# The order of 1,866 steps from a written list, and a last output tile in two column halves

## The chip, the cores and the metric

The kernel runs on one core of a Trainium2 chip. The metric is the device time of one execution in microseconds (us). Three executions of the kernel before took 486.77, 487.08 and 488.17 us; the median, 487.08 us, is the number that the prediction is about.

## What is computed

A gated linear recurrence, and behind it a two-layer block with the Mish activation. All data are float32.

```python
f = 1.0 / (1.0 + np.exp(-f_logit))                 # q, k, v, f_logit: (4, 8, 768, 48)
for t in range(S):
    state = f[:, :, t, :, None] * state + np.einsum('bhd,bhe->bhde', k[:, :, t], v[:, :, t])
    y[:, :, t] = np.einsum('bhd,bhde->bhe', q[:, :, t], state)
x = y.transpose(0, 2, 1, 3).reshape(3072, 384)
h = x @ w_in                                        # 384 x 2048
g = h * np.tanh(np.log1p(np.exp(np.minimum(h, 20.0))))
out = g @ w_out                                     # 2048 x 384
```

## The kernel before, in words

**The recurrence** is cut into 24 chunks (n0 to n23): 6 stretches of 128 time steps for each of 4 batches. A chunk is loaded on SP's queue (log-gates `l`, keys and queries `kq`, values `v`), prepared (L439 to L462: gates to running sums, their exponentials, and the products of k and q with them), and then goes through four stages: scores (L495) and masks (L508), a transposed copy of k called `kt`, the update of the state (L561), and the outputs (L632, L645). For the first eight chunks `kt` comes from TensorE transposes (L527) and a copy by ScalarE (L543). From chunk n8 on it goes by DMA: VectorE transposes blocks (L531), four DMAs write them to HBM (L536, `kd<-inv`), one reads them back (L538, `kt<-kd`), and one TensorE step, the run of that chunk (L595), does update, scores and outputs together.

**The two layers** work on 6 groups of 512 tokens (four chunks each) and 16 slices of 128 hidden columns: 96 units u0 to u95. A unit is nine 128x512 matmuls into `h` (`moe_in`, L256), eight elementwise steps on ScalarE, VectorE and GpSimd (`mish`, L270 to L278), and nine matmuls into the three output tiles `o0`, `o1`, `o2` (`moe_out`, L283). Every product is done as high and low parts, hence three matmuls for each. The weights of slice j are loaded (`raw`, 768 KB) and split into the parts `wh` and `wl` by ScalarE (L388, L395) and VectorE (L390 to L396).

**The order.** No engine's order is written in the loops. Each piece of work is entered with `add` as a step: its engine, a planned cost, what it reads and writes. There are 1,863 steps. `Plan.order` gives each a rank, shifts ranks at random with 71 listed seeds, and packs the steps by rank (`pack`); the steps are then issued in the order of their planned starts. So the order of instructions on TensorE (PE), VectorE (DVE), ScalarE (ACT), GpSimd (POOL) and of the DMAs on SP's queue comes out of that plan, and each engine works through its own list strictly in order. `Plan.issue` also puts filler matmuls (L376, on zeros) where the planned start of a TensorE step is more than 527 ns after the end of the one before it, up to the first `moe_out`.

**The end.** In the last unit, u95, each output tile gets its three matmuls (684 ns planned), then one copy to SBUF that multiplies by -2, by VectorE for tiles 0 and 2 (L797) and by ScalarE for tile 1 (L793), and one DMA of 256 KB (L799). The plan before puts tile 1 last.

Of the kernel before, what the change touches and what calls it, by code (L numbers as in the profile page):

```python
# [2 lines left out]

# [10 lines left out]
AF = mybir.ActivationFunctionType  # L14
ALU = mybir.AluOpType
# [4 lines left out]
P = 128  # L20
# [7 lines left out]
GT = GC * C  # L28
NG = NT // GT
NF = DFF // P  # L30
NK = DM // P
# [7 lines left out]
TURNS = [(0, 0, 8), (1, 0, 8), (0, 8, 16), (1, 8, 16)]  # L39

LEAD = [(-2, 8), (22, 32)]
SEEDS = [
# [8 lines left out]
]  # L51
BASE = (300.0, 20.0, 7)
NR = 3
LAG = 2
TD = 8
# [5 lines left out]
SP_ISSUE = 470  # L61
# [4 lines left out]
class Plan:  # L66
# [28 lines left out]
        lag = self.LATENCY[engine] if lag is None else lag  # L95
        self.steps.append((engine, cost, issue, before, size, port or engine == "pool", lag))

    def pack(self, rank, ahead, haste, back=False):


        steps = self.steps
        count = len(steps)
        engine, cost, port = [s[0] for s in steps], [s[1] for s in steps], [s[5] for s in steps]
        before = [s[3] for s in steps]
        after = [[] for _ in steps]
        for i in range(count):
            for b in before[i]:
                after[b].append(i)
        if back:
            before, after = after, before  # L110
        free = dict.fromkeys(self.FREE, 0.0) if back else dict(self.FREE)
        queue = {e: [] for e in free}
        left, ready, start = [len(b) for b in before], [0.0] * count, [0.0] * count
        for i in range(count):
            if not left[i]:
                queue[engine[i]].append(i)
        transfers = shared = 0.0
        for _ in range(count):
            best = None
            for e, q in queue.items():  # L120
                if q:
                    at = [(max(ready[i], shared) if port[i] else ready[i], i) for i in q]
                    t0 = max(free[e], min(at)[0])
                    _, t, i = min(
                        (rank[i] + haste * max(0.0, r - t0), max(free[e], r), i)
                        for r, i in at if r <= t0 + ahead
                    )
                    if best is None or t < best[0]:
                        best = t, i
            t, i = best  # L130
            e = engine[i]
            queue[e].remove(i)
            start[i] = t
            end = free[e] = t + cost[i]
            if port[i]:
                shared = end
            if e == "sp" and not back:
                transfers = max(transfers, end + 650.0) + steps[i][4] / self.RATE
                end = transfers - 650.0
            for a in after[i]:  # L140
                f = a if back else i
                if engine[i] == engine[a] == "pe":
                    lag = 0.0
                else:
                    lag = steps[f][6]
                    if back and engine[f] == "sp":
                        lag += steps[f][4] / self.RATE
                ready[a] = max(ready[a], end + lag)
                left[a] -= 1
                if not left[a]:  # L150
                    queue[engine[a]].append(a)
        return start

    @staticmethod
    def nudge(rank, seed):
        pick = random.Random(seed)
        lo, hi = min(rank), max(rank)
        at = lo + (hi - lo) * pick.random() ** 2
        width = (1e3, 3e3, 1e4, 4e4)[seed % 4]
        spread = (150.0, 500.0, 1500.0, 5000.0)[seed // 4 % 4]  # L160
        part = (1.0, 0.3, 0.1, 0.03)[seed // 16 % 4]
        return [
            r + pick.gauss(0.0, spread) if abs(r - at) <= width and (part == 1.0 or pick.random() < part) else r
            for r in rank
        ]

    def order(self):
        count = len(self.steps)
        cost = [s[1] for s in self.steps]
        ahead, haste, turns = BASE  # L170
        rank = list(range(count))
        for _ in range(turns):
            start = self.pack(rank, ahead, haste)
            back = self.pack([-start[i] - cost[i] for i in range(count)], ahead, haste, True)
            rank = [-back[i] - cost[i] for i in range(count)]
        for seed in SEEDS:
            rank = self.nudge(rank, seed)
        self.start = self.pack(rank, ahead, haste)
        return sorted(range(count), key=lambda i: (self.start[i], i))

    def issue(self):
# [19 lines left out]
def T_ACT(n, psum=False, bias=0):  # L201
    return n / 1.2 + (50 if psum else 92) + 93 * bias + 2


def T_DVE(n):
    return n / 0.96 + 70
# [7 lines left out]
def recurrence_moe_kernel(  # L214
# [11 lines left out]
    nc = tc.nc  # L226
# [10 lines left out]
    wih, woh = wh[:, :, : NK * P], wh[:, :, NK * P :]  # L237
# [40 lines left out]
            ("pool", T_POOL(GT), 1, lambda: nc.gpsimd.tensor_tensor(gl, g, gh.bitcast(F32), ALU.subtract)),  # L278
        )

    def moe_out(o, m, gh, gl, j, first, last, woh=woh, wol=wol):
        for i, (w, x) in enumerate(((woh, gh), (wol, gh), (woh, gl))):
            nc.tensor.matmul(  # L283
                o, w[:, j, m * P : (m + 1) * P], x, start=(first and i == 0), stop=(last and i == 2)
            )


    with tc.tile_pool(name="work", bufs=1) as pool, tc.tile_pool(
# [35 lines left out]
        def lender(m):  # L324
            return pairs(("ob", m)) + (pairs(("l", NR)) if m == 0 else thirds(("kq"[m - 1], NR)))
# [440 lines left out]
        def out_unit(u):  # L766
            t, g, j = units[u]
            half = g < 2
            first, last = (j == x for x in (turns[t][1], turns[t][2] - 1))
            part = last and half and j == NF - 1  # L770
            gs = u % 3
            if part:
                for m in range(NK):
                    add("sp", SP_ISSUE, lambda m=m, g=g: nc.sync.dma_start(ob_[m], halves[g][m * P : (m + 1) * P, :]),
                        [("half", g, m)], lender(m), 262)
            if u == 0:
                plan.until = len(plan.steps)
            if last or first:
                for m in range(NK):
                    add("pe", 684, lambda m=m: moe_out(o_[m], m, gh_[gs], gl_[gs], j, first, last),  # L780
                        [("w", "h", j), ("w", "l", j), ("gh", gs), ("gl", gs)], [("o", m)])
            else:
                add("pe", 2042, lambda: [moe_out(o_[m], m, gh_[gs], gl_[gs], j, first, last) for m in range(NK)],
                    [("w", "h", j), ("w", "l", j), ("gh", gs), ("gl", gs)], [("o", m) for m in range(NK)])
            if last:
                dst = halves[g] if j < NF - 1 else out[:, g * GT : (g + 1) * GT]
                for m in range(NK):
                    if part:
                        add("dve", T_DVE(GT), lambda m=m: nc.vector.scalar_tensor_tensor(
                            ob_[m], o_[m], -2.0, ob_[m], ALU.mult, ALU.add),  # L790
                            [("o", m)], lender(m))
                    elif m == 1:
                        add("act", T_ACT(GT, True), lambda m=m: nc.scalar.activation(ob_[m], o_[m], AF.Copy, scale=-2.0),  # L793
                            [("o", m)], lender(m))
                    else:

                        add("dve", T_DVE(GT), lambda m=m: nc.vector.tensor_scalar(ob_[m], o_[m], -2.0, None, ALU.mult),  # L797
                            [("o", m)] + ["flag"] * (u == len(units) - 1), lender(m))
                    add("sp", SP_ISSUE, lambda m=m, dst=dst: nc.sync.dma_start(dst[m * P : (m + 1) * P, :], ob_[m]),  # L799
                        lender(m), [("half", g, m) if half else ("out", g, m)], 262)  # L800

        add("act", 200, lambda: nc.scalar.activation(half_, ones, AF.Ln, bias=ones), (), ["half_"])
        add("act", 200, lambda: nc.scalar.activation(half_, half_, AF.Exp, scale=-1.0), (), ["half_"])
# [188 lines left out]
```

## Time and profile before

| | |
|---|---|
| three executions | 486.77, 487.08, 488.17 us |
| the profiled execution | 487.94 us, of which the span from first to last instruction is 486.2 us |
| PE busy | 475.5 us (98%), 4,824 matmuls, clock 0.998 of full speed |
| ACT busy | 395.9 us (81%) |
| DVE busy | 305.6 us (63%) |
| POOL busy | 133.1 us (27%) |
| DMA | 57.57 MB, mean 118 GB/s |

How to read it: shares are means over the whole span. They differ much between stages: the first 34 us are the first chunks and loads, the next 90 us have the most elementwise work beside the matmuls, and from some 200 us on the matmuls of the units make up nearly all that is left. A row of the timeline gives start, length, engine, line, operation, output<-inputs, shape and count, and in brackets the idle time of the engine before it and what ended it. PEld is TensorE's weight load. SPq is SP's queue, where a time is that of the issue and not of the transfer.

### The profile page before, as it was taken

The page shows a single profiled execution, that of the slowest core. Times are in us where ns is not written, and L with a number is a line of the kernel's source. Part 1 is how long each engine was busy: PE and PEld are TensorE (multiplying, and loading weights), DVE is VectorE, ACT ScalarE, POOL GpSimd, SP SyncE. Part 2 cuts the span into 40 slices and gives each one's busy share as a digit, 9 for nine tenths or more (in the row PEclk, how much of TensorE's full clock was granted, in tenths as well). Part 3 has the DMA queues.
Part 4 walks back from the last instruction along what each step waited for, and adds up shares of the span by engine and source line. Part 5 has one row for each costly group of instructions (what it writes and reads, how often), then busy time and mean ns, then how long its engine had stood idle before and what let it go on. Part 6 is the DMA issues. An engine that isn't in the chain of part 4 may idle for free.

```text
span 486.2 us, 11794 instructions
## 1 busy us (share of the span) xinstructions
PE 475.5 (98%) x4824; PEld 389.5 (80%) x4824; DVE 305.6 (63%) x523; ACT 395.9 (81%) x722; POOL 133.1 (27%) x125
## 2 busy tenths in 40 slices
PE   8899999999999999999999999999999999999995
PEld 7677778888888888788888888888888888888884
DVE  5799999999966777646637467636545433332221
ACT  7988999999998786887887878877787687778681
POOL 4322300000334232242233232332332323242422
PEclk9999999999999999999999999999999999999999
DMA  8975565534614744624325245213522000100001
GB/s 298 396 274 185 197 239 151 211 127 152 204 40 144 213 130 114 176 66 136 94 50 142 93 115 142 88 34 93 168 47 56 12 12 0 44 22 2 0 1 69
DMA packets 56604, 57.57 MB, mean 118 GB/s; under 512 B 36320, under 2 KB 39776, under 8 KB 56544
## 3 DMA queue, kind: packets, MB, share of 16 engines
q1 hardware_dynamic: 56544, 56.77, 37.5%
q8 instruction: 38, 0.62, 0.6%
q14 instruction: 22, 0.18, 0.1%
HBM read 43.25 MB, written 10.49 MB: 111 GB/s over the span
## 4 chain that ended last, share of the span: by engine, by line
PE 92%; DMA 3%; DVE 1%; SPq 1%; ACT 1%; issue 1%; DVEq 0%
PE h L256 40%; PE o L283 39%; PE at L645 3%; PE at L561 3%; PE at L632 2%; PE at L495 2%; DMA v<-vn 1%; PE o L376 1%; DMA kt<-kd 1%; PE at L527 1%; PE at L713 1%; SPq L536 1%; DMA kd<-inv 0%; DVE n L271 0%; DVE a L508 0%
## 5 line engine op out<-in xcount | busy, mean ns | idle before, releaser
L278 POOL TENSOR_TENSOR gl<-g,gh 128x512 fp32r<-128x512 f32 x80 | 106.1, 1328 | 286.8 <-ACT gh L276 268.2
L256 PE MATMUL h<-xt,wh 128*128 128x512 f32 x576 | 179.2, 392 | 0.0
L275 DVE SCALAR_TENSOR_TENSOR g<-n,half,h 128x512 f32<-128x512 f32 x96 | 71.5, 744 | 85.5 <-ACT n L274 81.2
L256 PEld LDWEIGHTS h<-xt,wh 128*128 128x128 f32 x576 | 106.9, 188 | 22.8 <-DVE g L275 0.4
L283 PE MATMUL o<-gh,wh 128*128 128x512 f32 x288 | 113.5, 394 | 0.0
L256 PE MATMUL h<-xt,wl 128*128 128x512 f32 x288 | 112.2, 390 | 0.0
L283 PE MATMUL o<-gl,wh 128*128 128x512 f32 x288 | 112.2, 390 | 0.0
L283 PE MATMUL o<-gh,wl 128*128 128x512 f32 x288 | 112.2, 389 | 0.0
L271 DVE TENSOR_SCALAR n<-n 128x512 f32<-128x512 f32 x96 | 47.5, 495 | 46.8 <-ACT n L270 46.3
L267 ACT ACTIVATE n<-n 128x512 f32<-128x512 f32 x96 | 60.4, 629 | 19.6 <-DVE n L271 19.1
L270 ACT ACTIVATE n<-h 128x512 f32<-128x512 f32 x96 | 56.6, 591 | 23.9 <-PE h L256 23.1
L276 ACT ACTIVATE gh<-g 128x512 fp32r<-128x512 f32 x96 | 60.2, 627 | 15.3 <-DVE g L275 15.2
L273 ACT ACTIVATE n<-n,ones 128x512 f32<-128x512 f32 x96 | 69.4, 723 | 2.5
L283 PEld LDWEIGHTS o<-gh,wh 128*128 128x128 f32 x288 | 54.0, 188 | 11.6
L283 PEld LDWEIGHTS o<-gl,wh 128*128 128x128 f32 x288 | 54.1, 188 | 11.5 <-POOL gl L278 0.2
L256 PEld LDWEIGHTS h<-xt,wl 128*128 128x128 f32 x288 | 54.1, 188 | 11.4
L283 PEld LDWEIGHTS o<-gh,wl 128*128 128x128 f32 x288 | 54.1, 188 | 10.8
L274 ACT ACTIVATE n<-n 128x512 f32<-128x512 f32 x96 | 60.3, 629 | 2.0
L332 DVE TENSOR_TENSOR kq<-kq,at 128x512 f32<-128x512 f32 (+1 forms) x38 | 25.2, 663 | 3.8 <-ACT at L458 3.1
L450 DVE TENSOR_TENSOR_SCAN cum<-go,l 128x512 f32<-128x512 f32 x20 | 24.9, 1246 | 0.8 <-ACT l L441 0.8
L561 PE MATMUL at<-v,kt 64*64 64x48 f32 x672 | 20.5, 219 | 1.6 <-DMA kt<-kd 0.9
L561 PEld LDWEIGHTS at<-v,kt 64*64 64x64 f32 x672 | 18.2, 135 | 4.4 <-issue 1.7
(135 smaller groups left out, 482.2 us busy)
## 6 DMA issues: line engine op xcount, KB each, us to landing
raw<-ww SPq DMA_DIRECT2D x16, 768.0 KB, 4.7
kq<-kq SPq DMA_DIRECT2D x23, 512.0 KB, 4.4
v<-vn SPq DMA_DIRECT2D x23, 256.0 KB, 5.1
l<-fl SPq DMA_DIRECT2D x20, 256.0 KB, 3.0
out<-ob SPq DMA_DIRECT2D x18, 256.0 KB, 2.3
kd<-inv SPq DMA_DIRECT2D x64, 64.0 KB, 2.2
kt<-kd SPq DMA_DIRECT2D x16, 256.0 KB, 2.7
xt<-xt SPq DMA_DIRECT2D x23, 128.0 KB, 2.6
```

What stands on the lines that cost most here:

```text
L256: nc.tensor.matmul(h, w[:, j, a * P : (a + 1) * P], xt[:, :, a, x, :], start=(n == 0), stop=(n == 3 * NK - 1))
L267: ("act", T_ACT(GT), 0, lambda: nc.scalar.activation(n, n, AF.Square))
L270: ("act", T_ACT(GT, True), 0, lambda: nc.scalar.activation(n, h, AF.Exp)),
L271: ("dve", 70 + GT / 1.92, 1, lambda: nc.vector.tensor_scalar(n, n, U_CAP, 1.0, ALU.min, ALU.add)),
L273: ("act", T_ACT(GT, False, 1), 0, lambda: nc.scalar.activation(n, n, AF.Ln, bias=ones)),
L274: ("act", T_ACT(GT), 0, lambda: nc.scalar.activation(n, n, AF.Exp, scale=-1.0)),
L275: ("dve", 662, 0, lambda: nc.vector.scalar_tensor_tensor(g, n, half_, h, ALU.subtract, ALU.mult)),
L276: ("act", T_ACT(GT), 0, lambda: nc.scalar.activation(gh, g, AF.Copy)),
L278: ("pool", T_POOL(GT), 1, lambda: nc.gpsimd.tensor_tensor(gl, g, gh.bitcast(F32), ALU.subtract)),
L283: nc.tensor.matmul(o, w[:, j, m * P : (m + 1) * P], x, start=(first and i == 0), stop=(last and i == 2))
L332: add("pool" if on_pool else "dve", cost, lambda: eng.tensor_tensor(dst, x, y, ALU.mult), reads, writes, port=port)
L561: return nc.tensor.matmul(u[c][half(e), p, :], kt[half(c), p, half(e)], moving, start=start, stop=True, skip_group_check=True,)
```

## The change

Two things. First, `pack`, `nudge`, the seeds and the ranks go; `ORDER` lists all steps by number, each engine takes its steps in the order of that list, and a replay computes planned starts from the same planned costs (they still decide where fillers stand). Second, tile 2 of the last unit is computed in two halves of 256 columns, each with its own three matmuls, its own copy (VectorE for the first, ScalarE for the second) and its own DMA of 128 KB. That takes three steps more, 1,866 in all. All other steps are the same work with the same numbers.

The numbers that matter below: 2, 41, 70 are the loads of `l` for n0, n1, n2; 3 and 42 those of `kq` for n0 and n1; 4 that of `v` for n0; 132 that of the first `raw`. Steps 225 and 156 are the second pass of the gates of n6 (L441) and the small end values of n4 (L459) on ScalarE; 155 is ScalarE's exponential for n4 (L458), 200 the high part of the second weight slice (L395), 161 the copy to `kt` of n4 (L543). Step 869 is VectorE's transpose of k for n13 (L531) and 833 its product g of unit u31 (L275). In the last row, 1853 is `moe_out` of u94, 1854 and 1855 are the matmuls of tiles 0 and 1, 1860 and 1861 those of the two halves of tile 2, 1856 to 1859 copy and DMA of tiles 0 and 1, 1862 and 1863 those of the first half, 1864 and 1865 those of the second.

```diff
-SEEDS = [
...
-BASE = (300.0, 20.0, 7)
+ORDER = [
+    2, 41, 70, 1, 3, 4, 42, 132, 5, 14, 6, 99, 15, 44, 7, 43, 45, 73,
...
+    199, 86, 153, 179, 87, 258, 107, 223, 40, 82, 154, 108, 88, 110, 109, 224, 89, 300,
+    111, 155, 62, 115, 69, 200, 121, 83, 112, 177, 158, 84, 116, 90, 114, 233, 201, 117,
+    95, 92, 234, 118, 93, 96, 180, 113, 119, 160, 120, 91, 259, 122, 235, 97, 94, 181,
...
+    869, 831, 1072, 875, 872, 855, 832, 871, 833, 870, 935, 860, 834, 873, 835, 858, 876, 788,
...
+    1832, 1828, 1833, 1840, 1834, 1841, 1842, 1835, 1838, 1843, 1836, 1844, 1837, 1848, 1845, 1846, 1847, 1853,
+    1860, 1854, 1862, 1861, 1863, 1856, 1855, 1864, 1857, 1858, 1865, 1859,
 ]
...
+    def order(self):
         steps = self.steps
         count = len(steps)
+        assert len(ORDER) == count
+        queue = {e: [i for i in ORDER if steps[i][0] == e] for e in self.FREE}
...
+            t, e = min(
+                (max(ready[q[0]], free[e], shared if steps[q[0]][5] else 0.0), e)
+                for e, q in queue.items() if q and not left[q[0]]
+            )
+            i = queue[e].pop(0)
+            _, cost, _, _, size, port, lag = steps[i]
+            self.start[i] = t
...
-    def moe_out(o, m, gh, gl, j, first, last, woh=woh, wol=wol):
+    def moe_out(o, m, gh, gl, j, first, last, woh=woh, wol=wol, cols=slice(0, GT)):
         for i, (w, x) in enumerate(((woh, gh), (wol, gh), (woh, gl))):
             nc.tensor.matmul(
-                o, w[:, j, m * P : (m + 1) * P], x, start=(first and i == 0), stop=(last and i == 2)
+                o[:, cols], w[:, j, m * P : (m + 1) * P], x[:, cols], start=(first and i == 0),
+                stop=(last and i == 2), skip_group_check=(cols.stop - cols.start < GT),
             )
...
+            whole = NK - (u == len(units) - 1)
...
+            if whole < NK:
+                m = whole
+                for x in range(2):
+                    cols = slice(x * GT // 2, (x + 1) * GT // 2)
+                    add("pe", 375, lambda cols=cols: moe_out(o_[m], m, gh_[gs], gl_[gs], j, first, last, cols=cols),
+                        [("w", "h", j), ("w", "l", j), ("gh", gs), ("gl", gs)] + [("part", 0)] * x, [("part", x)] + [("o", m)] * (1 - x))
+                for x in range(2):
+                    cols = slice(x * GT // 2, (x + 1) * GT // 2)
+                    o, ob, to = o_[m][:, cols], ob_[m][:, cols], dst[m * P : (m + 1) * P, cols]
+                    if x:
+                        add("act", T_ACT(GT // 2, True), lambda o=o, ob=ob: nc.scalar.activation(ob, o, AF.Copy, scale=-2.0),
+                            [("part", x)], [("obpart", x)])
+                    else:
+                        add("dve", T_DVE(GT // 2), lambda o=o, ob=ob: nc.vector.tensor_scalar(ob, o, -2.0, None, ALU.mult),
+                            [("part", x), "flag"], [("obpart", x)] + lender(m))
+                    add("sp", SP_ISSUE, lambda to=to, ob=ob: nc.sync.dma_start(to, ob), [("obpart", x)], [("out", g, m, x)], 131)
```

## Rows read from the trace of the kernel before

**Rows 1.** Stretches: length, busy PE, PEld, DVE, ACT, POOL; PEclk, DMA share, GB/s.
```profile
3.50:34.34 30.84, 28.29 (x573) 22.39 (x571) 23.50 (x42) 26.68 (x66) 10.24 (x15) 1.00 0.96 359
...
86.20:127.00 40.80, 40.80 (x239) 33.51 (x238) 39.76 (x64) 40.25 (x70) 2.75 (x2) 1.00 0.47 154
...
200.00:478.57 278.57, 278.48 (x2405) 230.14 (x2403) 136.65 (x241) 217.63 (x381) 85.69 (x70) 1.00 0.23 65
```
**Rows 2.** Timeline of all engines around 126 us.
```profile
125.45 0.75 DVE L275 SCALAR_TENSOR_TENSOR g<-n,half,h 128x512 f32<-128x512 f32 x1 [0.57 <-POOL gl L278]
...
126.25 0.19 PEld L256 LDWEIGHTS h<-xt,wh 128*128 128x128 f32 x1 [0.20 <-DVE g L275]
```
**Rows 3.** Chain of work that ended last, 180 to 200 us; start, length, what.
```profile
186.13 0.43 DVE g L275
...
187.50 1.12 DVE inv L531
...
191.51 2.16 DMA kd<-inv
...
193.75 3.27 DMA kt<-kd
```
**Rows 4.** Timeline of PE at 197 us.
```profile
197.07 0.25 PE L561 MATMUL at<-v,kt 64*64 64x48 f32 x1 [0.94 <-DMA kt<-kd]
```
**Rows 5.** Chain of work that ended last, the end of the span.
```profile
470.57 10.21 PE o L283 x45
```
**Rows 6.** Timeline of all engines at the end.
```profile
479.45 1.37 DVE L797 TENSOR_SCALAR ob<-o 128x512 f32<-128x512 f32 x2 [4.14 <-PE o L283]
...
480.81 0.60 ACT L793 ACTIVATE ob<-o 128x512 f32<-128x512 f32 x1 [4.77 <-PE o L283]
...
481.43 0.36 SPq L799 DMA_DIRECT2D out<-ob  x1
```
**Rows 7.** Timeline of SP's queue, the first issues.
```profile
2.13 0.43 SPq L386 DMA_DIRECT2D raw<-ww  x1
2.60 0.43 SPq L413 DMA_DIRECT2D kq<-kq  x1
```
**Rows 8.** Chain of work that ended last, the first 35 us.
```profile
3.08 7.28 DMA v<-vn
```
**Rows 9.** Timeline of ACT in the first 36 us.
```profile
8.34 0.62 ACT L543 ACTIVATE kt<-at 128x512 f32<-128x512 f32 x1
...
11.26 0.33 ACT L607 ACTIVATE mid<-at 128x192 f32<-128x192 f32 x1 [1.00 <-PE at L561]
...
17.23 0.60 ACT L458 ACTIVATE inv<-h 128x512 f32<-128x512 f32 x1 [0.90 <-PE h L445]
...
28.48 0.20 ACT L459 ACTIVATE ends<-cum 128x4 f32<-128x4 f32 x1
...
30.13 0.60 ACT L543 ACTIVATE kt<-at 128x512 f32<-128x512 f32 x1 [0.93 <-PE at L527]
30.62 0.71 ACT L441 ACTIVATE l<-l,ones 128x512 f32<-128x512 f32 x1
```
**Rows 10.** Timeline of SP's queue, the four `kd` DMAs of n11 and of n13.
```profile
158.85 2.57 SPq L536 DMA_DIRECT2D kd<-inv  x4
...
188.64 3.50 SPq L536 DMA_DIRECT2D kd<-inv  x4
```
**Rows 11.** Timelines of ACT, DVE and PE: operations on 256 columns.
```profile
14.00 0.38 ACT L715 ACTIVATE xt<-h 128x256 fp32r<-128x256 f32 x1
...
20.86 0.42 DVE L508 TENSOR_TENSOR a<-h,causal 128x256 f32<-128x256 f32 x1
...
74.43 0.40 PE L713 MATMUL at<-xt,minus 128*128 128x256 f32 x2
```
**Rows 12.** DMA issues by line; count, KB each, median us to landing.
```profile
out<-ob SPq DMA_DIRECT2D x18, 256.0 KB, 2.3
...
xt<-xt SPq DMA_DIRECT2D x23, 128.0 KB, 2.6
```

More of the change, by code (lines that the diff above doesn't have):

```diff
@@ L1 @@
-import random
 from contextlib import ExitStack
@@ L96, in add @@
         self.steps.append((engine, cost, issue, before, size, port or engine == "pool", lag))
-    def pack(self, rank, ahead, haste, back=False):
+    def order(self):
         steps = self.steps
         count = len(steps)
-        engine, cost, port = [s[0] for s in steps], [s[1] for s in steps], [s[5] for s in steps]
-        before = [s[3] for s in steps]
+        assert len(ORDER) == count
+        queue = {e: [i for i in ORDER if steps[i][0] == e] for e in self.FREE}
         after = [[] for _ in steps]
-        for i in range(count):
-            for b in before[i]:
+        for i, s in enumerate(steps):
+            for b in s[3]:
@@ L108, in pack @@
                 after[b].append(i)
[L109 to L117, printed above, removed]
-        for _ in range(count):
[L119 to L135, printed above, removed]
+        left, ready, self.start = [len(s[3]) for s in steps], [0.0] * count, [0.0] * count
@@ L136, in pack @@
+        free, transfers, shared = dict(self.FREE), 0.0, 0.0
+        for _ in range(count):
+            t, e = min(
[5 more added lines that the diff above has]
+            self.start[i] = t
+            end = free[e] = t + cost
+            if port:
                 shared = end
-            if e == "sp" and not back:
-                transfers = max(transfers, end + 650.0) + steps[i][4] / self.RATE
+            if e == "sp":
+                transfers = max(transfers, end + 650.0) + size / self.RATE
@@ L139, in pack @@
                 end = transfers - 650.0
             for a in after[i]:
[L141 to L148, printed above, removed]
-                left[a] -= 1
-                if not left[a]:
-                    queue[engine[a]].append(a)
@@ L152, in pack @@
[L152 to L178, printed above, removed]
+                ready[a] = max(ready[a], end + (0.0 if e == steps[a][0] == "pe" else lag))
@@ L777, in out_unit @@
                 plan.until = len(plan.steps)
+            whole = NK - (u == len(units) - 1)
             if last or first:
-                for m in range(NK):
+                for m in range(whole):
                     add("pe", 684, lambda m=m: moe_out(o_[m], m, gh_[gs], gl_[gs], j, first, last),
@@ L782, in out_unit @@
             else:
-                add("pe", 2042, lambda: [moe_out(o_[m], m, gh_[gs], gl_[gs], j, first, last) for m in range(NK)],
+                add("pe", 2042, lambda: [
+                    moe_out(o_[m], m, gh_[gs], gl_[gs], j, first, u == len(units) - 2 and m == NK - 1) for m in range(NK)],
                     [("w", "h", j), ("w", "l", j), ("gh", gs), ("gl", gs)], [("o", m) for m in range(NK)])
@@ L786, in out_unit @@
                 dst = halves[g] if j < NF - 1 else out[:, g * GT : (g + 1) * GT]
-                for m in range(NK):
+                for m in range(whole):
                     if part:
```

105 rows, old and new, of tables (ORDER, SEEDS) are left out of this document.

## Prediction, made before the change was run

> **What bounds the kernel now.** I read the stretches first, then the chain of waits, then the timelines where the chain leaves TensorE. From 200 us to the last unit PE is busy 278.48 of 278.57 us at full clock [rows 1]: no order of the same matmuls can win anything there. From 86 to 127 us PE is busy all of 40.80 us, and so, nearly, are ACT (40.25) and DVE (39.76) [rows 1]: three engines run full together. That PE is not far ahead is seen at 126 us, where its weight load for the next unit waits for VectorE's product g, which ends at 126.20, and starts 0.05 us behind it [rows 2]. So an earlier PE alone is worth little up to there; ACT and DVE have to be earlier too. Before 34.34 us, where the first unit starts, all engines have gaps: of 30.84 us ACT works 26.68 [rows 1], and the rest, 4.16 us, is what an order could win at the very most. The third place is one stall on a DMA: at 193.75 us the chain turns to the read-back of `kt` for n13, which lands at 197.02 [rows 3], and PE waits 0.94 us [rows 4]. The last place is the end: the matmuls are through at 480.78 [rows 5], ScalarE copies from 480.81 to 481.41, the last DMA is issued at 481.43 [rows 6], and the span ends at 486.2.
>
> **The change part by part.**
>
> *The head.* I laid the list beside the order before, queue by queue, and walked along the stalls.
>
> Loads: before, the values of n0 stand on SP's queue behind two l (192 KB each), kq of n0 (512), the first raw (768) and kq of n1 [rows 7] (512): with their own 256 KB that is 2,432 KB, and they land at 3.08 + 7.28 = 10.36 us [rows 8]. The list puts raw and the second kq behind them and a third l ahead: 1,344 KB. At the 359 GB/s of the stretch [rows 1] the 1,088 KB less are 3.0 us, so they land at about 7.3. The wait that takes its place is `kt` of n0: ScalarE's copy ended at 8.96 [rows 9], and the list puts one more exponential ahead of it (some 0.5 us). L561 of n0 so starts at about 9.6 instead of 10.49.
>
> ScalarE's idle 1.00 us ahead of its copy at 11.26 [rows 9] is then filled with work on n2, and the copy comes at about 10.8. Further on I price ScalarE's list one by one with the lengths of its rows, 0.5 to 0.6 us for 512 columns. Its next gap, 0.90 us ahead of 17.23 [rows 9], was a wait for TensorE's sums of n2; these move in front of an output stage, so the gap closes. The 0.93 us ahead of 30.13 [rows 9] was the transpose of n4, which came late since ScalarE's exponential for n4 (step 155) stood behind two copies of weights and the copy for n3; in the list it stands ahead of all of them, nearly 3 us earlier. Two of ScalarE's steps, 225 (0.71 at 30.62) and 156 (0.20 at 28.48) [rows 9], are put behind the point where the first unit can start; overlapped they are 0.7 to 0.8 us. The walk puts the copy of `kt` for n2 0.65 us earlier and the first unit at about 32.3: 2.0 us won.
>
> What of it stays is ScalarE's to say: 0.8 of the 2.0 is work put off, not saved, and has to be done before 127 us, in a stretch with 0.55 us of idle ScalarE [rows 1]. So ScalarE is some 1.2 us earlier, PE has a little slack beside it, and I take **-1.4**. Bounds: 0 below (the put-off work, a late load and the fillers can eat all), and 2.7 above (2.0 and the gaps that remain after it).
>
> *The stall at 195 us.* Its chain runs from VectorE: g of u31 from 186.13, the transpose from 187.50 to 188.62, four DMAs, their landing at 193.67, the read-back [rows 3]. In the list the transpose of n13 (869) stands ahead of that g (833): it starts some 0.7 us earlier, and the whole chain with it. PE stood still for 0.94 us [rows 4]. I take **-0.65**. Bounds: -0.94, since the four issues, which took 3.50 us here, took 2.57 for n11 [rows 10]; and 0, if other DMAs delay it again. For n11 the list goes the other way by about 0.2 us (a first min-and-add of u25 and a product for n9 ahead of its transpose, a partial sum less); PE did not wait for `kt` of n11 before, so I count nothing for it, with 0.2 above that at most.
>
> *The end.* The list does not put the halves last. It runs first half, tile 0, second half, tile 1: the whole tile 1 still ends the kernel, with ScalarE's copy of 512 columns and a DMA of 256 KB. Six matmuls of 256 columns take the place of three of 512. Two such matmuls behind each other took 0.40 us together [rows 11], each some 0.28 long, so their starts lie 0.12 apart: six are 0.72 us, where three of 512 columns at 0.227 (45 in 10.21 us [rows 5]) are 0.68. **+0.04**, and the bounds are 0 and +0.45 (each half held for a weight load's 0.19 us [rows 2]). VectorE's copy of the half costs 0.42 and ScalarE's 0.38 [rows 11], against 0.69 for the whole on VectorE (half of 1.37 [rows 6]). Both are hidden: the first runs while PE sums tile 0, the second while PE sums tile 1, and ends some 0.3 us before ScalarE is wanted for tile 1. Without that cover it would be 0.38 on the end. On SP's queue the fourth issue stands ahead of the last one; it is through, at 0.36 each [rows 6], about 0.2 us before tile 1 is copied. What is queued behind it is only the last DMA. The data are the same 768 KB.
>
> The Trainium skill speaks against such a split: "DMA: Bandwidth & Descriptors", Rules for kernel authors, says to coalesce many small transfers into a large one. The rows agree in so far as a transfer of 128 KB does not land sooner (2.6 us) than one of 256 KB (2.3) [rows 12]; no run here shows two halves against a whole.
>
> *Edits at no cost.* The two steps for the constant 0.5, moved from the start of ScalarE's list to about 11 us, ran before any load had landed. Seeds, packing and replay run before the kernel is built.
>
> **Sum.** -1.4 - 0.65 + 0.04 = -2.0 us against the profiled execution's 487.94 (486.2 of span and 1.7 around it): 485.9. The median of the three executions is 0.86 below the profiled one, so the forecast for the median is 487.08 - 2.0 = **485.1 us**. A measurement of this kernel can tell about 0.3%, 1.46 us, from no change.
>
> **Rivals.**
>
> *ACT and DVE hold PE back* (chance 0.27). The head ends earlier, but ScalarE, 0.8 us behind with put-off work, and VectorE deliver u8 to u20 as late as before, and PE stalls there for what it won. For it: the full stretch and the weight load that waits [rows 1, 2]. Against it: ScalarE's idle gaps in the head are real time, and they close. Then 0.3 of the head stays: 487.08 - 0.3 - 0.65 = 486.1.
>
> *SP's queue makes new stalls* (0.13), the one on the other side. 204 of its 219 issues before the last unit have another place, and the queue is strictly in order: a store that waits for a copy holds the `kd` and `kt` DMAs behind it. By the list, five runs (n10, n12, n13, n18, n20) follow their transpose by no more than four units of matmuls, 8.2 us; n13's chain needed 9.5 (187.50 to 197.02) [rows 3]. Each that goes like n13 costs about 1.1 us. From two on the gain is gone, with four it is 487.08 - 2.0 + 4 = 489.1. For it: one of those with such a lead stalled before. Against it: the four issues of n11 took 0.93 us less than those of n13 [rows 10], and a chain of 8.6 us costs next to nothing.
>
> *The halves are slow transfers* (0.08). If a half keeps the DMA engines as long as a whole tile, by the skill's rule above, four transfers of 0.7 us (three took the 2.1 us to the last data at some 375 GB/s) stand where there were three, and part of the fourth lies ahead of tile 1: +0.35 to +0.7, so 485.4 to 485.8. That the split does nothing for the time is part of my forecast and no rival.
>
> *My forecast* has 0.52, with its own range from 484.2 to 486.0.
>
> **How the numbers follow.** Faster by over 0.3% (below 485.62): 0.46 of the forecast's 0.52, 0.04 of the first rival, 0.03 of the third: 0.53. Slower by over 0.3% (above 488.54): 0.10 of the second and 0.02 for what I have not seen: 0.12. The rest, 0.35, is no difference. The range reaches down to 483.7 (2.7 won in the head and 0.7 at n13) and up to 488.0, two chains that stall anew and a head that gives half a microsecond.
>
> **What would show it.** Right: the values of n0 land near 7 us, ScalarE has no gap of 0.9 us behind 12 us, the first L256 starts near 32.3, the run of n13 waits for at most 0.4 us, the last copy is ScalarE's whole tile, with its issue as far behind the last matmul as before. Wrong: weight loads of L256 that wait for g from 60 to 127 us (first rival); L561 waits for `kt<-kd` of n10 to n20 (second); a last landing over 3.3 us behind its issue (third). The forecast fails most easily where ScalarE's put-off work comes due.

## The result, and the profile after

The changed kernel takes 491.25 us (median; 490.01 to 493.07), the kernel before, run beside it, 487.32 (486.77 to 488.71). The ratio is 1.0078, with a 95% interval from 1.0053 to 1.0102: slower by 0.8%, where 485.1 us was forecast. The profiled execution took 490.01 us, of which 488.2 are the span.

The stretches first, with the columns of [rows 1], cut where the changed kernel's first unit starts:

```profile
3.50:31.43 27.93, 25.60 (x565) 20.66 (x563) 21.59 (x42) 25.90 (x65) 9.66 (x14) 1.00 0.90 336
31.43:86.20 54.77, 53.46 (x704) 42.13 (x703) 51.81 (x85) 51.67 (x103) 7.94 (x8) 1.00 0.58 185
86.20:127.00 40.80, 39.39 (x351) 32.36 (x350) 38.98 (x61) 38.81 (x66) 2.59 (x2) 1.00 0.58 181
127.00:200.00 73.00, 72.90 (x794) 60.31 (x793) 49.09 (x89) 60.12 (x113) 22.89 (x20) 1.00 0.49 148
200.00:479.82 279.82, 277.23 (x2398) 228.97 (x2397) 132.36 (x239) 211.61 (x379) 85.52 (x70) 1.00 0.24 66
```

The head did shrink: the first unit starts at 31.43 instead of 34.34. But PE, which stood still for 0.09 us from 200 us to the last unit and not at all from 86 to 127 us before [rows 1], now stands still for 2.59 and 1.41 us there, and for 1.31 from 31 to 86 (0.49 before, from 34 on). The granted clock is 1.00 in all five stretches. What PE waited for, in total, times and longest:

```profile
PE at L603 <- DMA kt<-kd: 3.9, 4, 1.3
...
PE h L297 <- DVE g L316: 0.7, 1, 0.7
```

The four, in the timeline of PE (L603 is L561 of before):

```profile
88.48 0.68 PE L603 MATMUL at<-v,kt 64*64 64x48 f32 x32 [1.08 <-DMA kt<-kd]
...
124.61 0.25 PE L603 MATMUL at<-v,kt 64*64 64x48 f32 x1 [0.33 <-DMA kt<-kd]
...
231.73 0.25 PE L603 MATMUL at<-v,kt 64*64 64x48 f32 x1 [1.16 <-DMA kt<-kd]
...
291.06 0.22 PE L603 MATMUL at<-v,kt 64*64 64x48 f32 x1 [1.34 <-DMA kt<-kd]
```

They are the runs of n8, n9, n15 and n18; that of n13, the one that waited before [rows 4], waits no more. The chain from VectorE's transpose to the landing of `kt`, in us, for eight of the 16 chunks, read from the timelines of VectorE and SP and the landings:

```
         n8     n9    n12    n13    n15    n16    n17    n18
before  9.54   9.57   8.44   9.53   8.18   8.02   7.96   8.60
after  12.39  11.34   9.54   9.07  12.74  10.63   9.93  10.82
```

Of the other eight, n21 and n22 grew most, from 7.94 each to 10.86 and 9.82, but PE had no wait there. The transposes are not late; what follows them is. SP's queue at n15, changed kernel:

```profile
220.09 0.56 SPq L578 DMA_DIRECT2D kd<-inv  x1
220.73 0.57 SPq L455 DMA_DIRECT2D kq<-kq  x1
222.09 0.33 SPq L450 DMA_DIRECT2D l<-fl  x1
222.47 0.42 SPq L456 DMA_DIRECT2D v<-vn  x1
222.94 2.70 SPq L578 DMA_DIRECT2D kd<-inv  x3
228.96 0.33 SPq L580 DMA_DIRECT2D kt<-kd  x1
```

and in the kernel before:

```profile
222.26 2.63 SPq L536 DMA_DIRECT2D kd<-inv  x4
224.99 0.56 SPq L408 DMA_DIRECT2D l<-fl  x1
226.55 0.33 SPq L538 DMA_DIRECT2D kt<-kd  x1
```

Between the first and the last issue of `kd` the list puts three loads, 1,024 KB. They cost twice. On the queue: the load of `l` stands till 222.09 because its buffer is still read by VectorE, and three `kd` that are ready stand behind it; the chain shows it:

```profile
220.35 1.72 DVE cum L492
222.08 0.02 issue
222.09 0.33 SPq L450
222.42 0.05 issue
222.47 0.42 SPq L456
...
224.22 4.65 DMA kd<-inv
...
228.96 2.73 DMA kt<-kd
```

And on the DMA engines: the last `kd`, 64 KB, lands 4.65 us after its issue, behind the megabyte (before 2.15). The DMA view from 216 to 232 us gives the median from issue to landing, first the changed kernel, then the one before (the first of the four, issued ahead of the loads, landed in 2.08 us in the changed kernel):

```profile
kd<-inv SPq DMA_DIRECT2D x4, 64.0 KB, 4.8
```
```profile
kd<-inv SPq DMA_DIRECT2D x4, 64.0 KB, 2.2
```

Bytes between the first `kd` and `kt` are not the whole of it. At n8 the kernel before has the same 768 KB of weights there, and only their place differs. First the changed kernel, then the one before:

```profile
77.08 3.15 SPq L578 DMA_DIRECT2D kd<-inv  x3
80.34 0.65 SPq L428 DMA_DIRECT2D raw<-ww  x1
81.05 0.56 SPq L578 DMA_DIRECT2D kd<-inv  x1
85.81 0.34 SPq L580 DMA_DIRECT2D kt<-kd  x1
```
```profile
79.03 2.96 SPq L536 DMA_DIRECT2D kd<-inv  x4
82.09 0.56 SPq L386 DMA_DIRECT2D raw<-ww  x1
83.87 0.34 SPq L538 DMA_DIRECT2D kt<-kd  x1
```

Ahead of the last `kd` the load made it land 4.61 us after its issue, behind it 2.42, and the chain is 12.39 us instead of 9.54. At n18 the loads stand behind the last `kd` in both kernels, 512 KB instead of 256, and there `kt` is what lands late: 5.46 us after its issue instead of 3.31.

The end, all engines but PE; as predicted the last copy is ScalarE's whole tile:

```profile
482.06 0.60 ACT L837 ACTIVATE ob<-o 128x512 f32<-128x512 f32 x1 [0.31 <-PE o L324]
482.07 0.38 SPq L861 DMA_DIRECT2D out<-ob  x1
482.68 0.65 SPq L843 DMA_DIRECT2D out<-ob  x1
```

The matmuls end at 482.02 (before 480.77), and the span 6.2 us behind them (before 5.4). The last DMA landed 2.80 us behind its issue (before 3.21), so the 0.8 us more lie behind that landing: the span runs on for 2.7 us there, before for 1.5.

### The profile page after: what moved, and what is told of

Its sections match the earlier page's. It is cut to its first block, busy times and chain, and to the rows that moved or that the text cites. A ratio compares the mean times of both kernels' runs of the same rounds, so it can differ in the third digit from the quotient of the medians.

```text
span 488.2 us, 11763 instructions
## 1 busy us (share of the span) xinstructions
PE 473.1 (97%) x4817; PEld 387.7 (79%) x4817; DVE 297.1 (61%) x523; ACT 390.4 (80%) x723; POOL 131.5 (27%) x125
## 4 chain that ended last, share of the span: by engine, by line
PE 76%; DMA 9%; ACT 5%; DVE 5%; SPq 2%; issue 2%; POOL 0%; DVEq 0%; ACTq 0%; POOLq 0%
PE o L324 33%; PE h L297 32%; DMA kd<-inv 3%; DMA kt<-kd 3%; PE at L687 2%; PE at L603 2%; PE at L674 2%; PE at L537 2%; DMA raw<-ww 1%; DMA kq<-kq 1%; DMA l<-fl 1%; SPq L578 1%; DVE g L316 1%; DVE inv L573 1%; DVE cum L492 1%
## 5 line engine op out<-in xcount | busy, mean ns | idle before, releaser
L319 POOL TENSOR_TENSOR gl<-g,gh 128x512 fp32r<-128x512 f32 x80 | 104.3, 1306 | 294.6 <-ACT gh L317 283.9
L324 PE MATMUL o<-gh,wh 128*128 128x512 f32 (+1 forms) x289 | 113.3, 392 | 0.0
L324 PE MATMUL o<-gh,wl 128*128 128x512 f32 (+1 forms) x289 | 112.3, 389 | 0.0
L324 PE MATMUL o<-gl,wh 128*128 128x512 f32 (+1 forms) x289 | 112.3, 389 | 0.0
L312 DVE TENSOR_SCALAR n<-n 128x512 f32<-128x512 f32 x96 | 42.2, 439 | 58.5 <-ACT n L311 58.1
L324 PEld LDWEIGHTS o<-gl,wh 128*128 128x128 f32 x289 | 54.2, 188 | 11.3
L603 PE MATMUL at<-v,kt 64*64 64x48 f32 x672 | 20.3, 219 | 4.0 <-DMA kt<-kd 3.9
L603 PEld LDWEIGHTS at<-v,kt 64*64 64x64 f32 x672 | 18.1, 135 | 6.9 <-issue 3.1
```

What stands on the lines that cost most here:

```text
L312: ("dve", 70 + GT / 1.92, 1, lambda: nc.vector.tensor_scalar(n, n, U_CAP, 1.0, ALU.min, ALU.add)),
L324: nc.tensor.matmul(o[:, cols], w[:, j, m * P : (m + 1) * P], x[:, cols], start=(first and i == 0), stop=(last and i == 2), skip_group_chec ...
L603: return nc.tensor.matmul(u[c][half(e), p, :], kt[half(c), p, half(e)], moving, start=start, stop=True, skip_group_check=True,)
```

## Experiments

Of the theories, "the queue" says that the list's order of SP's issues behind the head makes `kt` late. The main rival says that ScalarE and VectorE give the head's gain back. The diffs are excerpts; `BEFORE` is the order of the kernel before, written as a list like `ORDER`. Inserted lists shift line numbers: L711, L710 and L713 below are L603. Ratios are to the kernel before, run beside each group; its medians were 487.65 (for the four kernels below the change), 487.88 (the next four) and 488.40 (the last three), so kernels of different groups are compared by ratio.

| kernel | median us | ratio, 95% |
|---|---|---|
| the change | 491.25 | 1.0078 (1.0053 to 1.0102) |
| list, last tile whole | 491.9 | 1.0072 (1.0044 to 1.0100) |
| list, SP's queue of before behind the head | 487.9 | 0.9994 (0.9973 to 1.0014) |
| list, `kd` and `kt` kept together | 501.07 | 1.0276 (1.0247 to 1.0304) |
| list's head, then before | 486.29 | 0.9963 (0.9945 to 0.9982) |
| the same, last tile whole | 486.61 | 0.9961 (0.9939 to 0.9983) |
| list's head, n15's chain as in the list | 487.39 | 0.9982 (0.9956 to 1.0008) |
| list's head, two loads behind `kt` | 486.13 | 0.9951 (0.9926 to 0.9975) |
| before's head, then the list | 490.74 | 1.0063 (1.0035 to 1.0091) |
| list, its SP order to n9 only | 489.16 | 1.0016 (0.9991 to 1.0041) |
| list, its SP order in the head and from n10 | 489.21 | 1.0014 (0.9994 to 1.0035) |
| two loads behind `kt`, n13 earlier | 485.85 | 0.9954 (0.9928 to 0.9980) |

**The tail undone.**

```diff
-            whole = NK - (u == len(units) - 1)
+            whole = NK
```

The last unit's steps stand in the order of before (tile 0, 2, 1).

> The list as it is, with the last tile whole again (tile order 0, 2, 1 as before; nothing else moves). Theory of the queue (the list's order on SP's queue makes TensorE wait four times for kt, 3.9 us in all, and that is what made the kernel slower): the four waits stay, and only the tail comes back. In the changed kernel the last matmul ended 6.2 us before the end of the span, in the kernel before 5.4 us, and the six half matmuls stand for 0.78 us where three whole ones took 0.68: at most 0.9 us less than the changed kernel, 490.4 against a median of 491.25. Rival, the split tail is the loss: 487.5 or less, and no stall elsewhere explains the rest.

Measured 491.9, the same as the change within the intervals, where 490.4 was expected at best; its span ended 6.0 us behind the last matmul too, and `kt` was waited for six times, 5.0 us (four times expected). The split tail is not the loss.

**SP's queue of before, behind the head.**

```diff
+        head = [i for i in ORDER[:207] if steps[i][0] == "sp"]
+        queue["sp"] = head + [i for i in BEFORE if steps[i][0] == "sp" and i not in head]
```

> The list for TensorE, VectorE, ScalarE and GpSimd, and on SP's queue only up to the first unit; behind that SP's issues stand in the order of the kernel before. Theory of the queue: the 2.9 us won in the head stay, the waits of L603 for kt shrink from 3.9 us to about 1, and the time is about 491.25 - 3 = 488.2, down to 487 if the waits for the weights (1.4 us in the changed kernel at 40 and 76 us) go too. Rival, ScalarE and VectorE give the head's gain back by themselves and the waits for kt are only where the lateness shows: the run of n8 starts as late as in the changed kernel, and the time stays within 1 us of 491.25.

Measured 487.9, 4.0 us less than the list with a whole tile in the same group. Its waits of PE:

```profile
PE h L405 <- DVE g L424: 1.5, 2, 0.9
...
PE at L711 <- DMA kt<-kd: 0.9, 2, 0.5
```

The time and the waits for `kt` are as expected. This kernel differs from the change in SP's order alone, and the ratio goes from 1.0078 to 0.9994: SP's order alone decides between slower and equal. The chain of n15 was 8.97 us, that of n18 8.01. But the waits for g are 1.5 us (0.7 in the change), the chains of n19 and n22 grew to 10.03 and 10.94, and the head's gain doesn't show. That a queue packed for other engine orders doesn't fit these either would explain it, but was not tried.

**The chains kept together.**

```diff
+VALUES = (810, 1000, 1069, 1138)
...
+        sp = queue["sp"]
+        for k in [i for i in sp if sum(steps[b][4] == KD_SIZE for b in steps[i][3]) == 4]:
+            kd = [i for i in sp if i in steps[k][3] and steps[i][4] == KD_SIZE]
+            a, z = sp.index(kd[0]), sp.index(k)
+            other = [i for i in sp[a:z] if i not in kd]
+            own = [i for i in other if i in VALUES]
+            sp[a : z + 1] = own + kd + [k] + [i for i in other if i not in own]
```

> The list on all engines; on SP's queue the four kd of a chunk and its kt stand behind each other, the loads and stores that the list put between them go behind the kt (the four loads of values of the same chunk go ahead of the first kd). Nothing else moves. Theory of the queue, in its narrow form (it is the transfers put between kd and kt that make them late): the chains of n8, n15 and n18, 12.4, 12.7 and 10.8 us from transpose to landing, come back to 8 to 9.5, the waits for kt from 3.9 us to under 1, and the time to about 488. In its wide form (the transfers that stand ahead of the four kd count as much, since they share the DMA engines): one to two of the four waits stay, about 489.5. Rival, the waits come from late transposes on VectorE: the waits stay at 3.9 us, 491.

Half right, and 10 us slower than the change. The chains of n8, n15 and n18 fell to 9.30, 9.13 and 8.02 us and the waits for `kt` to 0.5, so the narrow form holds for the chains. But the loads that went behind `kt` were needed at once. The waits of PE, and VectorE's timeline at n15:

```profile
PE h L305 <- DVE g L324: 8.4, 6, 3.4
...
PE at L611 <- DMA kt<-kd: 0.5, 1, 0.5
```
```profile
237.06 0.43 DVE L489 TENSOR_SCALAR l<-l 128x512 f32<-128x512 f32 x1 [4.39 <-DMA l<-fl]
```

VectorE stood for 4.39 us at the `l` whose load had been put behind `kt`, and g of the next unit stood behind it. In the list these loads are due too: its order on VectorE asks for them early, and in the two arrangements of its queue tried so far either `kt` or a load is late.

Not all of the 10 us are waits. Around PE's two longest waits, 2.32 us before 129.68 and 3.41 us before 241.52, the granted clock fell to 0.50, the lower of its two levels (1.2 GHz), once behind the wait and once within it:

```profile
131.07:134.48 3.41, 3.41 (x10) 2.63 (x9) 1.66 (x4) 3.29 (x6) 1.28 (x1) 0.50 0.00 0
240.30:247.13 6.83, 5.61 (x13) 4.45 (x14) 5.30 (x11) 6.06 (x14) 3.60 (x3) 0.50 0.00 1
```

A 128x512 matmul took 0.63 us there instead of 0.39. PE was busy for 477.3 us in this execution and for 473.1 in the change's, so by this estimate some 4 of the 10 us are the clock's. In the change's profile the clock fell only after the last matmul.

**The head of the list, the rest as before.**

```diff
+ORDER = ORDER[:207] + [i for i in BEFORE if i not in ORDER[:207]]
```

> The first 207 steps of the list (all that starts before the first unit's activations are planned to be through, about 35 us), and all other steps in the order of the kernel before; the tail split as in the changed kernel. Theory of the queue: the head's 2.9 us are kept but for the one stall at n13, 0.94 us, which stays, and the tail costs up to 0.9: about 487.3 - 2.9 + 0.6 = 485. Rival, ScalarE and VectorE limit TensorE up to 127 us and the head's gain is work put off: it is given back by then, the first units wait for g, and the time is 487 to 488.

Measured 486.29, 1.36 us under the kernel before in the same group, where 485 was expected: the head's gain is real and survives 86 to 127 us, where PE was busy all of 41.00 us. The rival falls for this order. 2.2 us of waits for `kt` are left (n13 and n18), more than the 0.94 of before.

**The same with the last tile whole.** The first diff and the last one together.

> As the run with the list's first 207 steps and the order of before behind them, with the last tile whole. In that run the split tail took 4.97 us from the last matmul's end to the end of the span, the kernel before 5.40, the changed one 6.21 and the list with a whole tile 6.04. Theory (what differs there is the spread of the last transfer, not the split): 486.3 plus or minus 0.5, no difference from the split one. Rival, the split costs time: 485.7 or less.

Measured 486.61: no difference. From the last matmul to the end of the span it was 5.25 us, against 4.97 with the split.

**One chain as in the list.**

```diff
+        sp, n15 = queue["sp"], [1024, 1068, 1284, 1000, 1021, 1023, 1022, 1025]
+        at = sp.index(1137)
+        queue["sp"] = [i for i in sp[:at] if i not in n15] + n15 + sp[at:]
```

> As the run with the list's first 207 steps and the order of before behind them; on SP's queue the chain of n15 alone stands as in the list: one kd, then the loads of kq for n16 (512 KB), of l for n19 and of the values of n15 (256 KB each), then three kd and kt. Theory of the queue: the chain of n15 grows from 8.4 us to about 12 (12.7 in the changed kernel), TensorE waits for kt of n15 for 12 - 8.4 - 2.7 of slack, that is 0.9 us, at 231 us, and the time is 0.9 over that run: about 487.2. Rival, the long chains in the changed kernel came from what was earlier on the queue (all loads pushed late), not from these three: chain under 9.5, no wait, 486.3.

The chain of n15 grew from 8.40 to 11.07 us (12 expected), so these three loads are what makes it long. Of that 1.6 us are issues (first to last `kd`) and 1.3 the landing of the last `kd`. The slack ahead of L603 fell from 2.69 to 0.13 us in the profiled execution, where PE so waited for no more than 0.1; the 0.9 expected did not come. The ratio is 0.19% (0.9 us) above that of the head's run, but the intervals overlap: the chain is shown, its price is not.

**Two loads behind `kt`.**

```diff
+        for load, kt in ((1136, 874), (1498, 1242)):
+            queue["sp"].remove(load)
+            queue["sp"].insert(queue["sp"].index(kt) + 1, load)
```

> As the run with the list's first 207 steps and the order of before behind them; the loads of l for n17 and n22 (256 KB each), which stand between the last kd and kt of n13 and of n18, go behind that kt. Both are wanted over 50 us later. Theory of the queue: kt of n18 lands 2.7 us after its issue instead of 4.55 and the wait there (1.05 less 0.04 between matmuls) goes; kt of n13 lands 0.6 us sooner, and its wait falls from 1.58 to about 1 or less: 1.5 us less in all, 484.8. Rival, the transfers' lengths vary from run to run whatever stands ahead: 486.3.

The waits for `kt` fell from 2.2 to 0.4 us, and the profiled span by 0.7; the ratio fell from 0.9963 to 0.9951 (0.6 us, 1.5 expected). That is not told apart from no change. `kt` of n18 still took 3.64 us to land instead of 4.55, not 2.7. That both loads are wanted 50 us later was wrong: VectorE's first pass over `l` waited for its loads for 8.1 us from 180 us on, 5.1 without this edit; only PE did not wait for it.

**The head of before, then the list.**

```diff
+ORDER = BEFORE[:195] + [i for i in ORDER if i not in BEFORE[:195]]
```

> The complement: the first 195 steps of the order before (up to 35 us of its plan), then the list; the tail split. Theory of the queue (the head's gain is real, and the list loses it again behind the head on SP's queue): the head ends as late as before, the waits for kt of n8 to n18 stay at about 4 us, and the time is 1 to 2 us over the changed kernel's 491.25: 492.2 to 493.2. Rival, the list's head itself makes the later waits, by putting work off: with the head of before they go, and the time is 487 to 488.

Neither. The time, 490.74, is that of the change within the intervals: the list behind the head costs its 0.6 to 0.8% whatever the head. The waits for `kt` are 2.3 us, not 4, and g was waited for once, 1.4 us at 111.5 us. The first unit starts at 34.26 here and at 31.43 in the change, but the run of n8 at 88.96 and 88.48: of 2.8 us, 0.5 are left. Between these two points PE stands still for 0.41 us here and for 2.39 in the change: 1.08 for `kt` of n8, 0.68 for g and 0.21 for a load of `xt`. So most of the head's gain is idled away up to the run of n8, about half of it at that chain, and the loss is not the sum of the parts.

**SP's order of the list in one half.** Up to the `kt` of n9:

```diff
+        sp = queue["sp"][: queue["sp"].index(655) + 1]
+        queue["sp"] = sp + [i for i in BEFORE if steps[i][0] == "sp" and i not in sp]
```

> The list on all engines; SP's queue follows the list up to the kt of n9 (its first 72 issues, about 121 us) and the order of the kernel before behind it. Theory of the queue, worked out by the waits of the changed kernel: the waits of the first 127 us stay (weights and g at 40 and 76 us 1.2 us, kt of n8 1.2, kt of n9 0.3), those of n15 and n18 (2.3 us) go: 491.25 - 2.3 = 489. Rival, one of the two halves makes all of the loss: 488 or less, or 491.

And the complement:

```diff
+        head = [i for i in ORDER[:207] if steps[i][0] == "sp"]
+        sp = head + [i for i in BEFORE if steps[i][0] == "sp" and i not in head]
+        sp = sp[: sp.index(655) + 1]
+        queue["sp"] = sp + [i for i in queue["sp"] if i not in sp]
```

> The list on all engines; SP's queue follows the list in the head (up to the first unit), then the order of the kernel before up to the kt of n9, and the list again from there. Theory of the queue: the waits for kt of n15 and n18 (2.3 us in the changed kernel) stay and those at 76, 87 and 124 us go; with the 487.9 of the run that has the order of before on SP's queue throughout this gives 487.9 + 2.3 = 490.2, and the two halves' surcharges add up to the 3.35 us between 487.9 and 491.25. Rival, the lateness is carried along the queue, so that the late part of the list does no harm without the early part: 488.

489.16 and 489.21 (489 and 490.2 expected), each about 1 us (0.22% and 0.20%) over the run with SP's queue of before, 0.9994. The waits stand where they should, at n8 in the first, at n15 in the second:

```profile
91.55 0.68 PE L711 MATMUL at<-v,kt 64*64 64x48 f32 x32 [1.55 <-DMA kt<-kd]
```
```profile
233.63 0.25 PE L713 MATMUL at<-v,kt 64*64 64x48 f32 x1 [1.78 <-DMA kt<-kd]
```

They are not the only ones: the first also waits for `kt` of n11 and n22, 0.39 and 0.97 us, where the run with SP's queue of before waits too (0.35 and 0.55), and the second for g, 1.56 us at 123 us. No half makes all of the loss. The wait at n15 comes without the early part of the list, so it isn't lateness carried over; the time alone can't tell that, since both intervals overlap that of the run with SP's queue of before. Together they would be 0.4% of the 0.8%; with intervals of a quarter of a per cent on each side that is no proof that they add up, nor that they don't.

**n13 earlier.** Beside the two loads:

```diff
+        queue["dve"].remove(833)
+        queue["dve"].insert(queue["dve"].index(869) + 1, 833)
```

> As the run with the loads of l for n17 and n22 behind their kt; on VectorE the product g of u31 (833) goes behind the transpose of n13 (869), as in the list, so that the transpose starts 0.66 us earlier. The prediction's second step alone: the wait for kt of n13 (0.66 in that run, 0.62 over what stands between matmuls otherwise) falls to nothing: 486.1 - 0.6 = 485.5. Rival, the earlier transpose gains nothing since the four kd still queue behind the loads ahead of them (four issues of 3.1 us instead of 2.3): 486.1.

No wait for `kt` is left in the profile (0.4 us before it), and the profiled span is 484.1, the shortest of all. The ratio, 0.9954, is that of the run without it, 0.9951: 0.6 us can't be told here. This version, the one without it and the two with only the list's head are the four whose intervals lie wholly below the kernel before, by 0.4 to 0.5% in the median, and they beat the change too.

## Why the prediction was wrong, step by step

**The head, -1.4: right in size where it stands alone, in part by luck.** The list's head ahead of the order of before won 1.36 us (0.9 to 2.7). In the change's profile the steps came as walked: L603 of n0 starts at 9.55 (9.6 said), ScalarE's longest gap from 12 us to the first unit is 0.32, and the first unit starts at 31.43 (32.3 said). Over the profiles of eleven kernels with this head the start lies from 31.43 to 33.88, median 33.15, and in three of them ScalarE has a gap of 1.00 to 1.08 us; two with the head of before give 34.34 and 34.26. So 31.43 was a lucky draw, and the walk too good: 2.0 us were forecast at the first unit, and the median is some 1.2. What ScalarE was to take back of it, 0.6, shows in no wait of PE. So two steps missed in opposite directions. The profile taken with the list's head alone, an execution of 487.55, doesn't show the gain at all: its matmuls end at 480.80, before at 480.77.

**The stall at n13, -0.65: right in place.** The transpose starts at 185.99 instead of 187.50, and PE waits for nothing; in the list with the last tile whole it still waits 0.46 us. On the whole time it could not be seen.

**The end, +0.04: right within the noise.** The six half matmuls took 0.35 and 0.43 us by their starts, 0.78 against 0.68: +0.10. Whole against split was measured twice without a difference. The third rival (the halves as slow transfers) falls by the same two runs; none showed the 0.35 to 0.7 that it priced, and the last landing, 2.80 us behind its issue, is below the 3.3 that were to be its sign.

**The edits at no cost, and the sum: this is where it failed.** SP's queue was charged nothing. The prediction saw that 204 of 219 issues moved, made that a rival, priced four stalls at 489.1 and gave it 0.13. That rival happened in kind: four stalls for `kt`, made by SP's queue. It did not happen as worked out. It had named n10, n12, n13, n18 and n20, and stores that wait; the trace has n8, n9, n15 and n18, and loads. Its 489.1 is 2.1 us short, since it counted the head's gain in full beside the stalls. And from 200 us on, where the prediction saw nothing to win, the change lost 2.5 us: an order that cannot win can lose. The rival was set aside by the wrong measure. I counted the lead, how many units of matmuls lie between a transpose and its run, found five short ones (n10, n12, n13, n18, n20), and took the chain's length as a constant of 8.6 to 9.5 us from the kernel before. The length is what the list changed: of the four that stalled only n18 is among the five, and n8, n9 and n15 have chains of 11.3 to 12.7 us. The step that was missing is to read, for each of the 16 chains, what the list puts on SP's queue and where: 768 KB ahead of the last `kd` at n8, 1,024 KB at n15. At the 359 GB/s of [rows 1] the megabyte is 2.9 us, and three issues of 0.43 each [rows 7] are 1.3 more: 4.2 by this estimate. The chain of n15 grew by 4.6: 2.1 from the first issue of `kd` to the last, of which 0.8 are the load that stood for its buffer, and 2.5 in the landing of the last `kd`. The estimate is no law: the same three loads made only 2.7 us in the run with the one chain.

**ACT and DVE holding PE back: not what made the loss.** With the list's head and the order of before, PE has no wait in the full stretch. The one wait for g in the change, 0.7 us at 40 us, is again a load's: that of `l` goes out as soon as VectorE's sum `cum` has left its buffer, and VectorE waits for it to land.

```profile
32.87 1.19 DVE cum L492
34.07 4.51 DMA l<-fl
38.60 0.41 DVE l L481
39.82 0.75 DVE g L316
40.61 2.32 PE h L297 x9
```

The sign that the prediction gave for this rival, waits for g between 60 and 127 us, is absent in the change but stands in three kernels with the list on VectorE and ScalarE behind the head: 1.43 us at 111.5 us, 0.63 at 122 and 1.56 at 123. In the last two the chain runs through the landing of a load of `raw` (6.46 and 7.37 us). What these engines would cost with all loads in time was not tried.

**Still open.** How the loss divides by cause. Two profiles add up. In the change's, an execution of 490.01, the first unit is 2.9 us earlier than before, PE stands still for 3.9 us more behind it (3.0 of them for `kt`), the span runs on 0.8 longer behind the matmuls, and 0.3 is left over: 2.1 us. But that is the fastest of seven executions, with the earliest start of the eleven. In the list with the last tile whole, profiled at 491.82, the first unit is 1.8 earlier, PE stands still for 4.8 more (4.1 for `kt`), 0.6 come behind the matmuls, and 0.2 is left over: 3.9 us, the loss of the medians. What each wait would give back by itself isn't shown, and the halves do not settle it.

## What to carry to other kernels

When an order is replaced, lay out the DMA queue chain by chain: for each write-out and read-back, what now stands ahead of its last write and of its read-back, in KB and in issues, and whether any of it waits for a buffer. A lead is only as good as the length of the chain that it has to cover. And time won early is only worth what is left of it at the next place where a queue, and not the engine, sets the time.

## What was not expected of the hardware

At n15 in the kernel before, four writes of 64 KB landed 2.15 to 2.18 us after their issue. In the changed kernel the one ahead of the megabyte of loads took 2.08, the three behind it on the same queue 5.22, 4.98 and 4.65. The Trainium skill says in "DMA: Bandwidth & Descriptors", section Two DMAs through the same engine are not ordered, that within one queue of one DMA engine descriptors start in order but are pipelined. The trace agrees in so far as the three writes behind the loads land late; the start of a single descriptor is not shown here.

The second half of the last tile waits for VectorE's copy of the first, though they share no column: the weight load for its first matmul stood idle for 0.25 us, until just behind the copy that ended at 480.65. This half took 0.08 us longer than the other. Whether the chip needs that wait, or the program alone asks for it, no run shows.

```profile
480.71 0.19 PEld L324 LDWEIGHTS o<-gh,wh 128*128 128x128 f32 x1 [0.25 <-DVE ob L859]
```
